# Weight operands kept in DRAM as one F32 part, split on load, with a respread decoding

## The chip, the cores and the metric

The kernel runs on one core of one Trainium2 chip. The metric is device time in microseconds, the median of the runs; less is better.

## The reference, cut to what matters

```python
# attention with decay: B=4, H=8, S=768, D=64, gamma[h] = 1 - 2**(-5-h)
for t in range(S):
    state = gamma[None, :, None, None] * state + np.einsum('bhd,bhe->bhde', k[:, :, t], v[:, :, t])
    y[:, :, t] = scale * np.einsum('bhd,bhde->bhe', q[:, :, t], state)
x = y.transpose(0, 2, 1, 3).reshape(B * S, H * D)        # 3072 x 512
h = (x @ w1) * (x @ w2)                                  # 512 -> 1024
x = h @ w3 @ w_out                                       # 1024 -> 1024 -> 512
h = x @ w_in                                             # 512 -> 2048
return (h * (1 / (1 + np.exp(-1.702 * h)))) @ w_out2     # 2048 -> 512
```

Inputs q, k, v are F32. The weights come as 64-bit floats and are decoded to F32 on the chip.

## The kernel before, in words

**Arithmetic.** A product is taken with three matmuls (`mm3`, L248 to L251): an operand is held as a high part, rounded to fp32r, and a low part, the residue, and high x high, high x low and low x high are summed. A split is a ScalarE cast and a VectorE subtraction (`split`, L263). The three large products behind the gates use seven block products in place of eight (P1 to P7): a 2 x 2 block operand is turned into seven operands by subtractions.

**Decoding.** `tiles` (L89) lists 36 weight tiles of 128 x 1024: 8 of w1 and w2, 4 of w_out, 8 of w3, and 16 of the FFN (w_in, then w_out2). Each half (512 columns) is fetched on SyncE's queue (`fetch`, 0.5 MB, `R_BUFS` = 4 buffers "r"), turned into a magnitude by ScalarE (`magnitude`, L114, 4 buffers "x"), then by VectorE through a clamp (L189), a shift (L198) and two bit merges (L202, L214). `weight_steps` is a generator with a yield after each step; `work(n)` takes n steps, as long as `done` is below `limit`. A tile of the first 20 is split into high and low on the chip and takes 10 steps. A tile of the FFN goes to `seven` (L158): POOL forms four differences (`four`, L144), ScalarE casts the seven parts, VectorE takes their residues (11 steps with these), and `store_parts` (L132) stores high and low parts to the DRAM tensors `sp` (w_in) or `sw` (w_out2), four stores on SyncE's queue.

**Stages.** Tokens are in six blocks of 512. (1) Attention, chunk by chunk, with the gates of block 0 between; decoding may take 86 steps here. (2) The mixed stage (loop at L989): for blocks n = 1 to 5 in `ORDER`, eight gates each (`gate_mm`, 24 matmuls of 512 columns), with PSUM for three gates. Between the gates of n = 1 and at the first of n = 2 stand eight rows of w3 @ w_out (`mix_mm`, 24 matmuls each); `mix_out` forms their seven parts per pair of rows, splits them, and stores them to `sm`. Decoding goes on: 8 steps per gate and 7 per row up to `limit` = 206 steps, then 5 per gate. Blocks 0 to 2 of `ORDER` store their gate products to `hd` (`gate_first`); blocks 3 to 5 read them back (`load_b`) and form five further operands by four POOL subtractions (L985), stored to `hd` on SyncE's queue (`gate_second`). In the last block `opening` loads the mixed weights, high and low, for each of the seven products, and the first operands of the next stage.

(3) The blend (`blend`, L783), 21 turns of 24 matmuls (three block pairs times seven products): `load_turn` fetches an operand of `hd` (1 MB, buffers "l", 3) on SyncE's queue two turns ahead, a split gives its high part (buffers "h", 2), TensorE multiplies, ScalarE, VectorE and POOL combine the results, which go to `yd` on SyncE's queue. `ahead` takes four decoding steps per turn while tiles are left; later it forms the operands of the next stage. (4) The expand (`Expand`, L525): left operands are the eight tiles of `sp`, fetched by POOL's queue (`fetch_left`, high and low, 1.8 MB each) into slots 0 to 7; four spans of 2 x 384 tokens, eight quads each, a quad being 42 matmuls of 384 columns; results go through the activation and to `gd`. (5) The contract (`contract`, L694), 21 turns of 48 matmuls: operands of `gd` are loaded and split per turn, weights of `sw` are loaded per product by `load_w`, high and low into two slots.

**Order.** The schedule is written by hand: each engine and each queue runs its instructions in the order in which the program gives them. A buffer with n copies is reused in turn, after the readers of its last content are done. A pool opened over another's room waits for what lay there.

## Time and profile before

| | us |
|---|---|
| median of 3 runs (lowest, highest) | 1085.14 (1082.16, 1089.9) |
| the profiled execution | 1086.86 |
| its span, first to last instruction | 1085.1 |
| TensorE busy in the span | 995.1 |
| VectorE, ScalarE, POOL busy | 715.4, 458.2, 186.9 |

The profile is of one execution. DMA moved 305.44 MB, a mean of 281 GB/s, and TensorE's mean granted clock was 0.964 of 2.4 GHz. The attention ends at about 150 us, the mixed stage runs from there to 439, the blend to 607, the expand to 852 and the contract to the end.

### The profile page before, as it was taken

What the parts mean: (1) busy time and instruction counts of PE and PEld (TensorE: products, weight loads), DVE (VectorE), ACT (ScalarE), POOL (GpSimd) and SP (SyncE); (2) the same over time, 40 slices, a digit from 0 to 9 for tenths busy, and PEclk for the clock granted to TensorE, in tenths of its full rate; (3) what the DMA queues carried; (4) which work ended last, traced back from release to release, by engine and by line L of the source; (5) the groups of instructions that cost most, each with busy time, mean ns of one, the idle gap of its engine ahead of it and who ended that gap; (6) DMA issues with size and microseconds to landing.
All of it is one profiled execution on the core that took longest, in us unless ns stands there. A gap on an engine that the chain in (4) does not pass through costs nothing.

```text
span 1085.1 us, 15024 instructions
## 1 busy us (share of the span) xinstructions
PE 995.1 (92%) x5608; PEld 852.0 (79%) x5608; DVE 715.4 (66%) x964; ACT 458.2 (42%) x831; POOL 186.9 (17%) x188
## 2 busy tenths in 40 slices
PE   4899899999999896568789889999999999999998
PEld 4788678778887774456577779999999888888886
DVE  5767768887799996338277238677677545455562
ACT  4556645444423332144434234544454543343340
POOL 3101000214377675314011100000000000000000
PEclk9999899999999997779899999999999999999999
DMA  8789947668899989998876695554659797887881
GB/s 309 244 315 342 338 170 236 222 218 275 324 367 323 379 320 394 415 343 275 282 234 199 262 414 232 214 233 192 231 215 367 296 371 241 290 300 261 283 269 62
DMA packets 140009, 305.44 MB, mean 281 GB/s; under 512 B 8480, under 2 KB 91552, under 8 KB 128544
## 3 DMA queue, kind: packets, MB, share of 16 engines
q1 hardware_dynamic: 133600, 253.89, 65.6%
q0 software_dynamic: 6336, 50.60, 12.3%
q8 instruction: 44, 0.72, 0.3%
q14 instruction: 29, 0.24, 0.1%
HBM read 183.87 MB, written 120.59 MB: 281 GB/s over the span
## 4 chain that ended last, share of the span: by engine, by line
PE 60%; DMA 19%; DVE 12%; issue 4%; ACT 4%; POOL 0%; SPq 0%; ACTq 0%; DVEq 0%; POOLq 0%
PE m L250 9%; PE m L251 8%; PE m L249 8%; DMA l<-hd 5%; PE a L249 4%; PE a L251 4%; PE a L250 4%; DMA raw<-in_wo_dram 4%; DMA xl<-xd 2%; DVE x L214 2%; PE e L251 2%; PE e L249 2%; PE e L250 2%; ACT h L264 2%; DVE x L202 2%
## 5 line engine op out<-in xcount | busy, mean ns | idle before, releaser
L249 PE MATMUL psm<-xh,wh 128*128 128x512 f32 x320 | 127.1, 397 | 15.3 <-ACT g L287 11.4
L250 PE MATMUL psm<-xl,wh 128*128 128x512 f32 x320 | 126.2, 394 | 0.0
L251 PE MATMUL psm<-xh,wl 128*128 128x512 f32 x320 | 126.0, 394 | 0.0
L249 PE MATMUL m<-h,op 128*128 128x512 f32 x320 | 124.5, 389 | 0.0
L251 PE MATMUL m<-h,op 128*128 128x512 f32 x320 | 124.5, 389 | 0.0
L250 PE MATMUL m<-l,op 128*128 128x512 f32 x304 | 118.3, 389 | 0.0
L664 ACT CAST h<-l 128x2048 fp32r<-128x2048 f32 x38 | 72.3, 1914 | 93.3 <-DMA l<-gd 49.2
L665 DVE TENSOR_TENSOR l<-l,h 128x2048 fp32r<-128x2048 f32 x38 | 85.8, 2286 | 28.6 <-ACT h L664 28.6
L249 PE MATMUL a<-yh,op 128*128 128x384 f32 x256 | 86.6, 338 | 7.9 <-ACT u L536 4.8
L250 PE MATMUL a<-yl,op 128*128 128x384 f32 x256 | 86.3, 337 | 0.0
L251 PE MATMUL a<-yh,op 128*128 128x384 f32 x256 | 86.3, 337 | 0.0
L249 PE MATMUL m<-h,wh 128*128 128x512 f32 x166 | 69.7, 420 | 17.8 <-ACT h L264 17.8
L249 PEld LDWEIGHTS psm<-xh,wh 128*128 128x128 f32 x320 | 61.0, 191 | 30.9 <-ACT g L287 12.2
L121 ACT ACTIVATE x<-raw 128x512 f32<-128x512 f32 x72 | 47.1, 673 | 90.3 <-DMA raw<-in_wo_dram 50.2
L156 DVE TENSOR_TENSOR l<-l,h 128x2048 fp32r<-128x2048 f32 x19 | 44.2, 2325 | 56.3 <-ACT h L264 56.3
L250 PE MATMUL m<-l,wh 128*128 128x512 f32 x152 | 62.8, 413 | 13.7 <-DVE l L156 13.6
L670 POOL DMA_DIRECT2D op<-sw x12 | 6.3, 528 | 399.5 <-PE a L251 222.0
L251 PEld LDWEIGHTS psm<-xh,wl 128*128 128x128 f32 x320 | 61.0, 191 | 13.1
L250 PEld LDWEIGHTS psm<-xl,wh 128*128 128x128 f32 x320 | 61.1, 191 | 12.5
L249 PEld LDWEIGHTS m<-h,op 128*128 128x128 f32 x320 | 60.1, 188 | 12.6
L251 PEld LDWEIGHTS m<-h,op 128*128 128x128 f32 x320 | 60.1, 188 | 12.3
L251 PE MATMUL m<-h,wl 128*128 128x512 f32 x166 | 68.6, 414 | 0.0
(147 smaller groups left out, 2222.8 us busy)
## 6 DMA issues: line engine op xcount, KB each, us to landing
gd<-g SPq DMA_DIRECT2D x32, 1344.0 KB, 5.1
qkv<-in_qkv_dram POOLq DMA_DIRECT2D x23, 1024.0 KB, 8.3
l<-gd SPq DMA_DIRECT2D x26, 768.0 KB, 7.1
l<-hd SPq DMA_DIRECT2D x19, 1024.0 KB, 6.6
raw<-in_w_dram SPq DMA_DIRECT2D x32, 512.0 KB, 5.3
hd<-g SPq DMA_DIRECT2D x12, 1280.0 KB, 6.8
op<-sp POOLq DMA_DIRECT2D x7, 1792.0 KB, 16.5
raw<-in_wo_dram SPq DMA_DIRECT2D x24, 512.0 KB, 8.6
```

What stands on the lines that cost most here:

```text
L121: nc.scalar.activation(x, high, AF.Abs, scale=2.0**16)
L156: nc.vector.tensor_tensor(lo, x, hi.bitcast(F32), ALU.subtract)
L202: nc.vector.scalar_tensor_tensor(bits, raw[:, :, 0], 29, bits, ALU.logical_shift_right, ALU.bitwise_or)
L214: nc.vector.scalar_tensor_tensor(bits, raw[:, :, 1], -(2**31), bits, ALU.bitwise_and, ALU.bitwise_or)
L249: nc.tensor.matmul(ps, wh, xh, start=start, stop=False, skip_group_check=True)
L250: nc.tensor.matmul(ps, wh, xl, start=False, stop=False, skip_group_check=True)
L251: nc.tensor.matmul(ps, wl, xh, start=False, stop=stop, skip_group_check=True)
L264: nc.scalar.copy(hi, x)
L664: nc.scalar.copy(hi, x.bitcast(F32))
L665: nc.vector.tensor_tensor(x, x.bitcast(F32), hi.bitcast(F32), ALU.subtract)
L670: queue.dma_start(t.bitcast(F32), sw[PART[name], :, w])
```

## The change

Weight parts go through DRAM as F32, undivided: `sp`, `sw` and `sm` lose their high and low halves. Where they are loaded, ScalarE and VectorE split them: left tiles in the first span of the expand (`split_left`), contract weights in every third turn (`split_w`), mixed weights at the last two gates and the first turns of the blend (`split_wm`). An FFN tile then has 8 steps; `limit` is lifted at the start of the mixed stage, and the steps per gate are 8 up to n = 2, 3 for n = 3 and 4, and 1 for n = 5. There are five raw buffers (three in use from n = 4 on, so that the operand h1 fits into two), six "x" and four "l" buffers. Stores of parts, of g and of yd move from SyncE's queue to POOL's; two of the four subtractions of `gate_second` move from POOL to VectorE, one of them to the gate before. The next block's x is loaded at gates 0 and 1 and split at 4 to 7.

```diff
-R_BUFS = 4
+R_BUFS = 5
...
-    sp = spool("sp", NQ, P, 2, 7 * 256)
-    (sw,) = spool("sw", 1, 7, P, 2, NQ, 256)
-    (sm,) = spool("sm", 1, 7, P, 2, NM, 256)
+    sp = spool("sp", NQ, P, 7 * 256)
+    (sw,) = spool("sw", 1, 7, P, NQ, 256)
+    (sm,) = spool("sm", 1, 7, P, NM, 256)
...
-    def fetch(n):
-        i, c = divmod(n, 2)
-        if i >= len(tiles):
+    fetched = used = 0
+    allowed = R_BUFS
+    def fetch():
+        nonlocal fetched
+        if fetched >= min(used + allowed, 2 * len(tiles)):
             return
+        i, c = divmod(fetched, 2)
+        fetched += 1
...
-            x = prep.tile([P, WC], F32, tag="x", bufs=4, name="x")
...
+            x = prep.tile([P, WC], F32, tag="x", bufs=6, name="x")
...
-    def store_parts(i, m, hi, lo):
-        a, b = (0, 3) if m == 0 else (3, 7)
-        for n, x in enumerate((hi, lo)):
-            x = x[:, : (b - a) * 256]
+    def store_parts(i, a1, a2, st):
+        for a, x in ((0, a1), (2, a2[:, 256:]), (3, st)):
+            b = a + x.shape[1] // 256
             if WI <= i < WI + NQ:
-                to = sp[i - WI][:, n, a * 256 : b * 256]
+                to = sp[i - WI][:, a * 256 : b * 256]
...
                 to = (sm, i) if i < WI else (sw, i - WI - NQ)
-                to = to[0][a:b, :, n, to[1]].rearrange("r p c -> p r c")
+                to = to[0][a:b, :, to[1]].rearrange("r p c -> p r c")
                 x = x.rearrange("p (r c) -> p r c", c=256)
-            nc.sync.dma_start(to, x.bitcast(F32))
+            nc.gpsimd.dma_start(to, x)
...
-    def seven(i):
...
+    def seven(i, a1, a2):
+        st = homes["st"].tile([P, 1024], F32, tag="st", bufs=2, name="st")
         four(st, a1, a2)
-        h0, l0, h1, l1 = (tile(F32R) for _ in range(4))
-        nc.scalar.copy(h0[:, :512], a1)
-        nc.scalar.copy(h0[:, 512:768], a2[:, 256:])
-        def last():
-            nc.scalar.copy(h1, st)
-            residue(h1, l1, st)
-            store_parts(i, 1, h1, l1)
-        def second():
-            residue(h0[:, 512:768], l0[:, 512:768], a2[:, 256:])
-            store_parts(i, 0, h0, l0)
-        return [lambda: residue(h0[:, :512], l0[:, :512], a1), second, last]
+        store_parts(i, a1, a2, st)
...
                     upper(i, n)
-                elif n:
-                    lows[:] = seven(i)
-                fetch(2 * i + n + R_BUFS)
-                yield i
+                used += 1
+                fetch()
+                fetch()
+                magnitude(i + 1)
+                if i >= WI and n:
+                    seven(i, *wx[i])
+                yield i + (i >= WI and n)
...
     def fetch_left(n, queue=nc.gpsimd):
...
+        t = left[n][:, 1].rearrange("p b c -> p (b c)")
+        queue.dma_start(t.bitcast(F32), sp[n])
+    def split_left(n):
+        hi, lo = (left[n][:, w].rearrange("p b c -> p (b c)") for w in range(2))
+        split(hi, lo, lo.bitcast(F32))
...
             next(fourth)
+            if s == 0 and j + 2 < NQ:
+                split_left(j + 2)
...
             self.results = [self.result(j) for j in range(2)]
+            split_left(1)
...
-    def load_w(name, w, at, queue=nc.gpsimd):
+    def load_w(name, at, queue=nc.gpsimd):
         t = slot(at, [P, NQ, 256])
-        ws.setdefault(name, []).append(t)
-        queue.dma_start(t.bitcast(F32), sw[PART[name], :, w])
+        ws[name] = [None, t]
+        queue.dma_start(t.bitcast(F32), sw[PART[name]])
+    def split_w(name, at, a=0, b=NQ, copy=nc.scalar.copy):
+        if a == 0:
+            ws[name][0] = slot(at, [P, NQ, 256])
+        hi, lo = (x[:, a:b] for x in ws[name])
+        copy(hi, lo.bitcast(F32))
+        nc.vector.tensor_tensor(lo, lo.bitcast(F32), hi.bitcast(F32), ALU.subtract)
...
     OPENING = {(n + 1, 1): [lambda n=n: opening_slot(n)] for n in range(4)}
+    OPENING[5, 1] = [lambda: load_w("P1", 4)]
     for n in range(2):
-        OPENING[5 + n, 1] = [lambda n=n: load_w("P1", n, 4 + n)]
+        OPENING[6, 1 + 2 * n] = [
+            lambda n=n: split_w("P1", 5, n * KH, n * KH + KH, nc.vector.tensor_copy)
+        ]
...
             if i == 0 and r + 1 < 7:
-                for w in range(2):
-                    queue = nc.gpsimd if r else nc.sync
-                    load_w(turns[n + 3][0], w, (6, 4)[r % 2] + w, queue)
+                load_w(turns[n + 3][0], (6, 4)[r % 2], nc.gpsimd if r else nc.sync)
...
             split_turn(n + 1, p)
+            if i == 1 and r + 1 < 7:
+                split_w(turns[n + 2][0], (7, 5)[r % 2])
...
-    def load_h(n, t):
+    def load_h(n, a, b, t):
         i, name = blends[n]
-        lo2[n] = t
-        nc.sync.dma_start(t.bitcast(F32), hd[i][:, :, RIGHT[name]])
...
+        lo2.setdefault(n, []).append((a, b, t))
+        nc.sync.dma_start(t.bitcast(F32), hd[i][:, a:b, RIGHT[name]])
+    def low_h(n, k):
+        return next(t[:, k - a] for a, b, t in lo2[n] if a <= k < b)
+    def split_h(n, a, b, hi):
+        for c, d, t in lo2[n]:
+            c0, d0 = max(a, c), min(b, d)
+            if c0 < d0:
+                lo = t[:, c0 - c : d0 - c]
+                split(hi[:, c0 - a : d0 - a], lo, lo.bitcast(F32))
+    wm = {}
+    def split_wm(n):
+        hi, lo = wm[blends[n][1]]
         split(hi, lo, lo.bitcast(F32))
...
             wm[name] = wtile("wg")
...
+            nc.sync.dma_start(
+                wm[name][1].bitcast(F32), sm[PART[name]].rearrange("p k c -> p (k c)")
+            )
...
             hi2[0] = x[:, NM:]
-            load_h(0, x[:, :NM])
-            load_h(1, prep.tile([P, NM, TB], F32R, tag="h1", name="h1"))
+            load_h(0, 0, NM, x[:, :NM])
+        if t == KF - 2:
+            for k in (0, 2):
+                load_h(1, k, k + 2, prep.tile([P, 2, TB], F32R, tag="r", bufs=R_BUFS, name="h1"))
         if t in (4, 5, 6):
-            split_h(0, t - 4)
+            split_h(0, t - 4, t - 3, hi2[0][:, t - 4 : t - 3])
+        if t in (6, 7):
+            split_wm(t - 6)
...
             if n < len(blends):
-                load_h(n, tile("l", 3))
+                load_h(n, 0, NM, tile("l", 4))
...
         def store(i, e, t):
-            nc.sync.dma_start(yd[i][:, e], t)
+            nc.gpsimd.dma_start(yd[i][:, e], t)
...
         load_turn(2)
-        hi2[1] = tile("h", 2)
+        hi2[1], k3 = tile("h", 2), tile("h", 2)[:, 0]
+        load_turn(3)
...
         ready = [value()]
-        k3 = p.tile([P, TB], F32R, name="k3")
-        split(k3, lo2[0][:, 3], lo2[0][:, 3].bitcast(F32))
+        split_h(0, 3, 4, k3.rearrange("p (a t) -> p a t", a=1))
...
             if n:
-                load_turn(n + 2)
+                load_turn(n + 3)
...
                         k3 if (n, k) == (0, 3) else hi2[n][:, k],
-                        lo2[n][:, k],
+                        low_h(n, k),
...
                     hi2[n + 1] = tile("h", 2)
-                split(hi2[n + 1], lo2[n + 1], lo2[n + 1].bitcast(F32))
+                split_h(n + 1, 0, NM, hi2[n + 1])
+            if n + 2 < 7:
+                split_wm(n + 2)
...
             pb = stage.enter_context(tc.tile_pool(name="b1", bufs=1, reuse_waits="tile"))
-            homes["wa"] = homes["wc"] = pb
-            limit = TILE_OPS * WI + 6
+            homes.update(dict.fromkeys(("wa", "wc", "st"), pb))
+            limit = ALL
...
                 if f % 2 == 0:
-                    pair = pb.tile([P, 2, 2, 256], F32, tag="xp", name="xp")
+                    pair = pb.tile([P, 2, 2, 256], F32, tag="xp", bufs=2, name="xp")
                 nc.scalar.copy(pair[:, :, f % 2], ps.rearrange("p (m f) -> p m f", m=2))
-                if f % 2 == 0:
-                    return
-                a1, a2 = (pair[:, m].rearrange("p a f -> p (a f)") for m in range(2))
-                st = pb.tile([P, 1024], F32, tag="st", name="st")
-                four(st, a1, a2)
...
-                    for r, x in todo:
-                        split(hi[:, r], lo[:, r], x)
-                    store_parts(f // 2, m, hi, lo)
-                pieces(0, [(slice(512), a1), (slice(512, 768), a2[:, 256:])])
-                later.append(lambda: pieces(1, [(slice(1024), st)]))
+                if f % 2:
+                    seven(f // 2, *(pair[:, m].rearrange("p a f -> p (a f)") for m in range(2)))
...
             def gate_second(t, i, ab):
-                nonlocal b12
+                nonlocal b12, g
+                b = hb[0]
...
                     b12 = pb.tile([P, TB], F32, tag="b", bufs=2, name="b12")
+                    g = pb.tile([P, 5, TB], F32, tag="g", bufs=2, name="g")
                     gate_out(b12, ab)
+                    nc.vector.tensor_tensor(g[:, 1], b12, b[:, 0], ALU.subtract)
                     return
-                g = pb.tile([P, 5, TB], F32, tag="g", bufs=2, name="g")
                 gate_out(g[:, 0], ab)
-                b = hb.pop(0)
-                for x, y, z in (
-                    (1, b12, b[:, 0]),
-                    (2, g[:, 0], g[:, 1]),
-                    (3, g[:, 0], b12),
-                    (4, b[:, 1], g[:, 2]),
-                ):
-                    nc.gpsimd.tensor_tensor(g[:, x], y, z, ALU.subtract)
-                nc.sync.dma_start(hd[i // 2][:, t // 2, 2:], g)
-            b12 = pb2 = None
+                nc.vector.tensor_tensor(g[:, 3], g[:, 0], b12, ALU.subtract)
+                nc.gpsimd.tensor_tensor(g[:, 2], g[:, 0], g[:, 1], ALU.subtract)
+                nc.gpsimd.tensor_tensor(g[:, 4], b[:, 1], g[:, 2], ALU.subtract)
+                nc.gpsimd.dma_start(hd[i // 2][:, t // 2, 2:], g)
+                hb.pop(0)
...
                         opening(t)
-                    elif 1 <= t <= KD:
-                        reload(nxt, t - 1)
+                    elif t < 2:
+                        for d in range(2):
+                            reload(nxt, 2 * t + d)
...
                     ab = gate_mm(t, i, gate_tile)
-                    if nxt is not None and 3 <= t < 3 + KD:
-                        split_x(nxt, t - 3)
-                    end = t >= KF - 3 and nxt is None
-                    for _ in range(5 if pb2 else 8):
-                        before = complete
-                        work(1)
-                        if end and complete > before:
-                            limit = done
+                    if nxt is not None and t >= KD:
+                        split_x(nxt, t - KD)
+                    if n >= 4 and t > 2:
+                        allowed = R_BUFS - 2
+                    work((1 if nxt is None else 3) if n > 2 else 8)
                     (gate_second if n > 2 else gate_first)(t, i, ab)
...
                         if rows == KF:
-                            later.pop()()
                             stage.close()
-                            pb = pb2 = stage.enter_context(
+                            pb = homes["st"] = stage.enter_context(
...
                             )
-                            homes["wa"] = pb
-                            limit = ALL
...
             nonlocal py, early
+            if n == len(blends) - 2:
+                split_left(0)
```

## Rows read from the trace of the kernel before

**Rows 1.** The page, 40 slices of 27.1 us: TensorE busy, DMA busy, in tenths
```profile
PE   4899899999999896568789889999999999999998
...
DMA  8789947668899989998876695554659797887881
```

**Rows 2.** Windows by stage: us, busy us of each engine (instructions), PEclk, DMA, GB/s
```profile
151.00:288.00 137.00, 133.78 (x581) 109.94 (x582) 109.76 (x189) 63.27 (x106) 26.15 (x28) 0.99 0.72 250
288.00:440.00 152.00, 136.66 (x579) 110.64 (x578) 134.88 (x147) 49.51 (x84) 102.57 (x83) 0.94 0.96 352
439.00:607.00 168.00, 130.70 (x503) 101.14 (x503) 90.49 (x79) 63.97 (x66) 29.78 (x25) 0.89 0.79 277
607.00:661.00 54.00, 46.09 (x244) 45.06 (x243) 19.26 (x36) 19.82 (x44) 3.17 (x6) 0.94 0.92 375
661.00:852.00 191.00, 191.00 (x1104) 191.00 (x1103) 139.82 (x255) 94.02 (x210) 1.06 (x2) 1.00 0.62 239
```

**Rows 3.** Windows, instructions on tile m alone, late blend and contract
```profile
540.00:607.00 67.00, 60.49 (x261) 48.26 (x260) 5.12 (x8) 7.62 (x14) 1.00 0.61 200
852.00:1081.00 229.00, 228.68 (x1008) 189.17 (x1008) 20.00 (x29) 7.06 (x12) 1.00 0.79 267
```

**Rows 4.** Chain that ended last, in order of time: start, us, what
```profile
444.10 9.59 DMA sw<-ws
...
453.77 19.36 DMA l<-hd
...
547.64 6.22 DMA l<-hd
...
607.84 9.00 DMA op<-sp
```

**Rows 5.** Waits in the blend: who for whom, us, times, longest
```profile
PE m L249 <- ACT h L264: 17.8, 6, 7.7
...
PE m L250 <- DVE l L156: 13.6, 9, 1.8
...
ACT h L264 <- DMA l<-hd: 47.2, 11, 11.0
```

**Rows 6.** Lines of VectorE, 152 to 182 us: group xcount | busy us, mean ns
```profile
L202 DVE SCALAR_TENSOR_TENSOR x<-raw,x 128x512 int32<-128x512 int32 x8 | 5.1, 682 | 0.0
...
L198 DVE TENSOR_SCALAR x<-x 128x512 int32<-128x512 int32 x8 | 3.0, 418 | 0.0
```

**Rows 7.** Lines of VectorE, 300 to 400 us
```profile
L202 DVE SCALAR_TENSOR_TENSOR x<-raw,x 128x512 int32<-128x512 int32 x14 | 16.7, 1227 | 0.0
...
L198 DVE TENSOR_SCALAR x<-x 128x512 int32<-128x512 int32 x14 | 14.1, 1040 | 0.0
```

**Rows 8.** DMA issues: op xcount, KB each, us to landing
```profile
l<-hd SPq DMA_DIRECT2D x19, 1024.0 KB, 6.6
...
op<-sp POOLq DMA_DIRECT2D x7, 1792.0 KB, 16.5
...
sp<-ws SPq DMA_DIRECT2D x16, 512.0 KB, 7.5
```

**Rows 9.** Lines of the whole span
```profile
L664 ACT CAST h<-l 128x2048 fp32r<-128x2048 f32 x38 | 72.3, 1914 | 93.3 <-DMA l<-gd 49.2 <-PE m L251 41.8 <-DVE l L665 2.3
...
L665 DVE TENSOR_TENSOR l<-l,h 128x2048 fp32r<-128x2048 f32 x38 | 85.8, 2286 | 28.6 <-ACT h L664 28.6
...
L153 POOL TENSOR_TENSOR ws<-x 128x256 f32<-128x256 f32 x32 | 29.5, 922 | 86.5 <-DVE x L214 59.4 <-issue 20.2 <-ACT ws L167 4.9
...
L985 POOL TENSOR_TENSOR g<-h,g 128x512 f32<-128x512 f32 x12 | 19.9, 1661 | 0.0
...
L156 DVE TENSOR_TENSOR xl<-xl,xh 128x512 fp32r<-128x512 f32 x20 | 14.8, 739 | 7.5 <-ACT xh L264 7.3
...
L330 POOL DMA_DIRECT2D qkv<-in_qkv_dram x25 | 14.0, 562 | 100.1 <-ACT state L386 25.4 <-PE y L408 21.3 <-ACT wh L125 18.1
```

**Rows 10.** Timeline of SyncE's queue: start, us, what
```profile
464.99 13.78 SPq L142 DMA_DIRECT2D sw<-ws  x2
```

More of the change, by code (lines that the diff above doesn't have):

```diff
@@ L116, in magnitude @@
             return
-        wx[i] = []
-        for raw in raws[i]:
-            x = prep.tile([P, WC], F32, tag="x", bufs=4, name="x")
+        xs = wx.setdefault(i, [])
+        for raw in raws.get(i, [])[len(xs) :]:
+            x = prep.tile([P, WC], F32, tag="x", bufs=6, name="x")
             high = raw[:, :, 1].bitcast(F32)
             nc.scalar.activation(x, high, AF.Abs, scale=2.0**16)
-            wx[i].append(x)
+            xs.append(x)
     def upper(i, n):
@@ L204, in weight_steps @@
                 )
-                yield i - len(rest)
-            for f in rest:
-                f()
                 yield i
@@ L518, in fetch_left @@
     def fetch_left(n, queue=nc.gpsimd):
-        t = left[n]
-        queue.dma_start(t.rearrange("p a b c -> p a (b c)").bitcast(F32), sp[n])
+        t = left[n][:, 1].rearrange("p b c -> p (b c)")
[3 more added lines that the diff above has]
+        split(hi, lo, lo.bitcast(F32))
     def left_parts(n, name, k):
@@ L770, in opening @@
             wm[name] = wtile("wg")
-            for w, x in enumerate(wm[name]):
-                nc.sync.dma_start(
-                    x.bitcast(F32), sm[PART[name], :, w].rearrange("p k c -> p (k c)")
-                )
+            nc.sync.dma_start(
+                wm[name][1].bitcast(F32), sm[PART[name]].rearrange("p k c -> p (k c)")
+            )
         if t == 1:
@@ L922, in tile_kernel @@
             psw = mixed_bank()
-            later = []
             rows = 0
@@ L1014, in tile_kernel @@
                         work(7)
-                        while later:
-                            later.pop()()
                         mix_out(rows, ps)
@@ L1019, in tile_kernel @@
                         if rows == KF:
-                            later.pop()()
                             stage.close()
-                            pb = pb2 = stage.enter_context(
+                            pb = homes["st"] = stage.enter_context(
                                 tc.tile_pool(name="b2", bufs=1, reuse_waits="tile")
                             )
-                            homes["wa"] = pb
-                            limit = ALL
         inner.close()
-        limit = ALL
-        homes["wa"] = second.enter_context(
+        homes["st"] = second.enter_context(
             tc.tile_pool(name="wa", bufs=1, side="right", reuse_waits="tile")
```

35 lines of the change are left out of this document (11 added, 24 removed).

## Prediction

> **What bounds the kernel now.** I read the page's slices first: TensorE is at 9 nearly everywhere but the start, a stretch in the middle and a few single slices, and the dip lies where DMA is at 8 to 9 [rows 1]. Next come windows by stage [rows 2] and the pace where nothing waits, the contract: 228.68 us for 1008 matmuls [rows 3], 0.227 us each, so 5.44 us for the 24 matmuls of a gate, a mixed row or a blend turn. The expand's pace is 191 us for 1104 [rows 2], 0.173 each, 7.27 us a quad of 42. Against these paces the stages lose:
> - 151 to 288 us (16 gates and 8 mixed rows of blocks n = 1 and 2, 24 x 5.44 = 130.7): 137 - 130.7 = 6.3;
> - 288 to 440 (24 gates, n = 3 to 5): 152 - 130.7 = 21.3, at a DMA share of 0.96;
> - 439 to 607 (blend, 21 turns, 114.3): 53.7;
> - 607 to 661 (244 matmuls, 5.8 quads, 42.2): 11.8. From 661 us on, nothing.
> Together 93.1 us; a change in the middle can win no more.
>
> What ends last there: the chain in order of time passes from a store of weight parts (9.59 us) into the blend's first loads of hd (19.36), later from load to load (6.22), and into the expand by a load of left parts of 9.00 us [rows 4]. In the blend TensorE waits for splits by ScalarE (17.8) and VectorE (13.6), and ScalarE in turn 47.2 us for the loads [rows 5]. SyncE's queue is part of it: one pair of stores of parts, whose data was late, held it 13.78 us while the next load stood behind [rows 10]. So the bound from 288 to 660 us is transfers and the queue in front of them, with VectorE close behind (134.88 of 152 us busy [rows 2]).
>
> **The change, part by part.** *Traffic.* A tile of seven parts is 128 x 1792 F32, 0.92 MB; it went out and came back twice over and now goes once: 16 tiles to sp and sw and 4 to sm, both ways, 40 x 0.92 = 36.7 MB less. Per gate in n = 3 and 4 before: 5 of 11 steps, 0.45 tile x (1.05 read + 1.84 stored) = 1.31 MB, and g, h and x 1.05 MB: 2.36 MB in 5.44 us, 433 GB/s, against 352 reached [rows 2]; n = 5 also fetched two operand tiles per mix. After, a tile has 8 steps and a gate 3 of them: 0.37 x 1.97 + 1.05 = 1.78 MB, 328 GB/s; n = 5 (one step, half the mixed weights, two hd loads) 1.63 MB, 299 GB/s. Both lie below what the stage reaches now.
>
> *VectorE and POOL in n = 3 to 5.* The two residues of a tile leave VectorE, two subtractions per pair of gates come to it at 0.74 each [rows 9], and POOL loses those two at 1.66 [rows 9]. The two engines slow each other: the same shifts and ORs take 418 and 682 ns where POOL rests [rows 6], 1040 and 1227 where it is busy [rows 7]. VectorE per gate: 3 steps x 0.55 to 1.13, two products and a subtraction and half a split together 1.9: 3.6 to 5.3 us, inside 5.44 even at the dear end. I leave 4 us of the 21.3 (0 if all fits, 12 if stores and g still collide): gain 17.
>
> *Blocks n = 1 and 2.* The limit on decoding falls. By the step counts (86 done in the attention, 8 per gate, 7 per row) eight FFN tiles are now decoded in n = 2, one per gate, where three were. Per gate VectorE has 4 x 0.42 + 4 x 0.68 = 4.4 plus 1.05 for a product and a half split: 5.5 us; with all steps as dear as in rows 7 it is 4 x 1.04 + 4 x 1.23 + 1.05 = 10.1. POOL has four subtractions at 0.92 and three stores at 0.56 [rows 9], 5.4 us. DMA has 2.36 MB, 433 GB/s again. An x buffer now stays taken until its store has landed, 3.7 + 0.6 + 7.5 [rows 8] = 11.8 us after the tile, and six buffers want it back after two tiles. I take 6.3 us, near the cheap end, since POOL no longer works on g in this block: 8 x 0.86 = 7 us behind, of which the three pairs of PSUM banks hide most; 4 reach TensorE (none to 8 x 4.7 - 10.9 = 26). The mixed rows lose four splits of ScalarE and VectorE each pair: 2 back. The stage then loses 8: gain -2.
>
> *Blend.* Decoding is over but for two steps (before, seven turns carried it). The operand load is issued three turns ahead over four buffers, on a queue with no stores: it has 10.9 us for a landing of 6.6 [rows 8], and the 47.2 us of waits should go. What is late next is the split: a copy out of PSUM of 0.6, cast 1.91 and residue 2.29 [rows 9] follow the end of a turn, 4.8 us and the signals, against 5.44. So 21 turns cost between 5.44 and what the late turns cost now, 67 x 24 / 261 = 6.16 [rows 3]; I take the middle, 5.8, 121.8 us. The mixed weights' splits (ScalarE half of 1.91 and VectorE half of 2.29 in turns 0 to 4) fit beside it: ScalarE then has 4.1 of 5.44, VectorE 5; without that cover they cost up to 5 x 1.1. One wait is new: k3 now takes the second "h" buffer, so the operand of turn 2 gets the one that turn 1 reads, and its split starts when turn 1 ends: 4.9 once (nothing, if that turn's load is late anyway). Left over 12.4 of 53.7: gain 41 (24 to 50).
>
> *Expand.* Left tiles 1 to 6 are 5.5 MB instead of 11. But the split of tile 1 stands on ScalarE ahead of quad 0's copies. Tile 1 landed after 9.00 us [rows 4], the middle one after 16.5 [rows 8]; at half the bytes I estimate 5.5. Then the cast of 1792 columns, 7/8 of 1.91, 1.7 us, and a copy of 0.5: TensorE, done with P1 and P5 after 2.1, waits until 7.7 + 0.6 (issue) = 8.3, 6.2 us lost, where 2.7 were lost before. The other 9 us, late tiles and stores of g held up at 375 GB/s [rows 2], fall to about 2. The later splits (1.7 of ScalarE, 2.0 of VectorE in a quad of 7.27 in which they are busy some 3.6 and 5.3 [rows 2]) fit. Left over 8.5 of 11.8: gain 3 (-3 to 8).
>
> *Contract.* A split of 1.91 and 2.29 in every third turn: 191 us of the expand and all of the contract run without loss and with both engines below 0.75 busy; the split is due two turns ahead. Nothing, and at most 6 x 0.5 without cover. *Startup.* A fifth raw buffer asks for 0.5 MB more beside the first qkv loads: 1.4 us at 370 GB/s lost, or as much won later from being further ahead; nothing, give or take 2.
>
> *Store queue.* Stores move to POOL at 0.56 us an issue [rows 9], in order with its arithmetic. The operands' stores wait there for POOL's own results, and behind them stand only POOL's next tile and g. In n = 3 to 5 POOL has 7 x (3.7 + 1.7) + 12 x (3.3 + 0.6) = 85 of 131 us.
>
> **The sum.** -2 + 17 + 41 + 3 = 59, with 1 us less of low clock after stalls (0.89 granted in the blend [rows 2]) 60. The profiled execution took 1086.9 (1.8 around its span of 1085.1), the median of the runs is 1085.1, 1.7 below; 1085 - 60 = **1025 us**. About 1% is what a measurement of this kernel tells from no change.
>
> One rule speaks against the new queue. By the Trainium skill (SBUF — State Buffer, "A bandwidth-pool intuition that's wrong (but worth ruling out)"), a DMA issued by POOL can take 3.1 us instead of 0.62 beside a VectorE copy, since its descriptors wait for the shared port. By that price the third rival below would come out at 1111 us. This trace disagrees so far: 25 issues by POOL beside decoding took 562 ns in the mean [rows 9], but those are loads, and no row has a store.
>
> **Rivals.**
> *The blend keeps its pace.* The split chain of 4.8 us plus signals, not the loads, sets the turn, and the first loads come late because their buffers lie over g, whose last store must land first. Turns of 6.16 [rows 3] and 10 us at the start: 129.4 + 10 + 4.9 = 144, 18 more than forecast: 1043. For it: 13.6 us of waits for VectorE in nine short pieces [rows 5]. Against: those fell in turns whose load was late.
> *Block n = 2 is overloaded.* VectorE at 10.1 us a tile: 26 instead of 4: 1047. For it: rows 7. Against: there POOL was 102.57 of 152 us busy [rows 2], mostly with g.
> *POOL's queue sets the pace, and the kernel is slower.* If a store takes s us of POOL, n = 2 has 8 x (3.7 + 3s) against 43.5 and 10.9 of slack, and n = 3 to 5 have 65.7 + 33s against 130.7; the loss is 57s - 90, which eats the gain from s = 2.6 on; at s = 3 it is 81 us: 1106. For it: stores have up to 512 pieces instead of 128. Against: 0.56 [rows 9], and left loads of 256 pieces cost POOL no more.
> *The transfers were hidden anyway*, and only order changes: n = 3 to 5 are held by POOL and VectorE, and half the blend's loss stays: 1060. Against: 0.96 DMA share [rows 2] and the chain [rows 4].
>
> **Chances.** Forecast 0.66, blend's pace 0.13, n = 2 0.09, hidden transfers 0.07, POOL's queue 0.05. The range goes from 1004 (blend 50, n = 3 to 5 all 21, expand 8, first blocks 2) to 1060, which holds the first two rivals and leaves out the last, and what lies above the one before. Faster by over 1% (below 1074): all cases but POOL's queue, less a little, 0.92; within 1% 0.03; slower 0.05.
>
> **What would show it.** Right: DMA share from 288 to 440 us at about 0.8, gates of 5.44; no decoding beside the blend and ScalarE's wait for hd near 5 us; turn 2 late by 5; a stall of 6 us in quad 0, none from quad 1 on; contract unchanged; total traffic near 269 MB. Wrong: TensorE waiting in n = 2 for the products' VectorE steps, POOL DMA issues far above 0.6 us, or VectorE's residue still behind TensorE in every blend turn.

## Result and the profile after

The changed kernel takes 1016.72 us (median of four runs, 1016.0 to 1019.8), the kernel before 1085.39 in the same comparison: ratio 0.937, 95% interval 0.9331 to 0.9409. That is 68.7 us less, where 60 were forecast, inside the range. The profiled execution took 1016.0 us with a span of 1014.2, and TensorE's mean granted clock rose from 0.964 to 0.984.

The page of the kernel after: 40 slices of 25.4 us, TensorE busy, its granted clock and DMA in tenths, what DMA moved, and the chain's shares by engine.

```profile
PE   4999999999989999899997999999999999999998
...
PEclk9899999999989999999997999999999999999999
DMA  8789956569999977998846745546497978767871
...
DMA packets 115032, 268.73 MB, mean 265 GB/s; under 512 B 7952, under 2 KB 69520, under 8 KB 105488
...
PE 82%; DVE 5%; DMA 4%; POOL 4%; issue 3%; ACT 2%; POOLq 0%; DVEq 0%; ACTq 0%; SPq 0%
```

Against [rows 1] the dip in the middle is gone. Four notches are left, at slices 12, 17, 22 and the start; slice 12 is block n = 3's first gates, slice 17 (406 to 431 us) the blend's first turn, slice 22 (533 to 558) the expand's first quad. The traffic is the 269 MB of the forecast, 36.7 less than before. On the chain of work that ended last, transfers fell from 19% to 4% and TensorE rose from 60% to 82%.

Windows by stage, with the columns of [rows 2]: n = 1 and 2; the first 10 us of n = 3; n = 3 to 5 and what follows them up to the blend; the blend's first turns; the rest of the blend; the first of the expand.

```profile
147.00:278.00 131.00, 131.00 (x578) 108.37 (x579) 117.22 (x190) 51.37 (x89) 59.01 (x70) 1.00 0.74 252
278.00:288.00 10.00, 5.37 (x17) 3.65 (x16) 10.00 (x16) 2.85 (x6) 6.36 (x9) 0.74 1.00 365
278.00:415.00 137.00, 132.37 (x573) 108.78 (x572) 110.88 (x130) 32.90 (x58) 89.37 (x96) 0.98 0.88 320
415.00:440.00 25.00, 19.90 (x80) 15.67 (x79) 19.74 (x18) 12.61 (x14) 11.51 (x12) 0.93 0.96 362
440.00:537.00 97.00, 97.00 (x429) 80.07 (x428) 69.22 (x51) 48.93 (x45) 23.18 (x29) 1.00 0.72 249
537.00:591.00 54.00, 46.74 (x254) 46.34 (x253) 32.32 (x44) 31.17 (x52) 3.68 (x7) 0.91 0.68 261
```

Waits of TensorE from 147 to 600 us, as in [rows 5]: who for whom, us in total, times, longest.

```profile
PE a L232 <- ACT s L523: 7.3, 1, 7.3
PE m L233 <- DVE h L160: 4.0, 1, 4.0
PE psm L232 <- ACT xh L247: 3.6, 1, 3.6
PE m L233 <- DVE l L160: 1.1, 1, 1.1
PE psm L233 <- DVE xl L160: 1.0, 1, 1.0
```

Between three single stalls (278 to 288, at 415, at 538) TensorE hardly waits: 131.00 us busy of 131 for the first 24 gates and rows, where the pace alone asks 130.7, and 97.00 of 97 us busy in the late blend, 429 matmuls, 5.43 us per 24. Where ScalarE waited 47.2 us for hd in the blend [rows 5], the same group has 2.2 now.

The stages of each run, in one profiled execution: the attention up to the first gate matmul behind it, each later stage up to the start of its last matmul. The last columns are the median of all runs and its ratio to the kernel before. This table carries the experiments below; two profiles with the same code in a stage differ by up to 3 us there (the expand of e1 and of the changed kernel).

| kernel | attention | mixed | blend | expand | contract | median | ratio |
|---|---|---|---|---|---|---|---|
| before | 150.9 | 287.7 | 168.8 | 244.7 | 228.5 | 1085.39 | |
| after | 146.9 | 268.6 | 121.9 | 243.7 | 228.4 | 1016.72 | 0.937 |
| e1 | 146.0 | 278.4 | 122.2 | 240.9 | 228.5 | 1025.01 | 0.9441 |
| e2 | 146.8 | 285.7 | 138.1 | 246.3 | 228.5 | 1053.35 | 0.9706 |
| e3 | 145.5 | 274.6 | 123.5 | 243.5 | 228.5 | 1022.75 | 0.9422 |
| e4 | 145.8 | 271.5 | 129.8 | 242.9 | 228.4 | 1024.93 | 0.9448 |
| e10 | 147.0 | 268.5 | 123.3 | 242.8 | 228.5 | 1019.05 | 0.9393 |
| e5 | 147.0 | 269.2 | 122.2 | 243.4 | 228.4 | 1013.60 | 0.9336 |
| e6 | 147.0 | 268.9 | 120.4 | 250.9 | 228.5 | 1023.18 | 0.9423 |
| e8 | 147.7 | 266.0 | 126.7 | 242.6 | 228.4 | 1016.91 | 0.9362 |
| e9 | 150.3 | 280.7 | 122.1 | 243.3 | 228.5 | 1031.32 | 0.9503 |
| e7 | 147.3 | 277.6 | 126.0 | 242.3 | 228.5 | 1028.15 | 0.9464 |
| b1 | 151.0 | 308.4 | 150.1 | 246.2 | 228.5 | 1089.44 | 1.0025 |
| e12 | 146.6 | 270.2 | 126.5 | 240.4 | 228.5 | 1018.66 | 0.9382 |

### The profile page after: what moved, and what is told of

Its sections match the earlier page's. It is cut to its first block, busy times and chain, and to the rows that moved or that the text cites. A ratio compares the mean times of both kernels' runs of the same rounds, so it can differ in the third digit from the quotient of the medians.

```text
span 1014.2 us, 14850 instructions
## 1 busy us (share of the span) xinstructions
PE 971.7 (96%) x5608; PEld 841.1 (83%) x5608; DVE 727.0 (72%) x954; ACT 448.8 (44%) x793; POOL 209.8 (21%) x254
## 4 chain that ended last, share of the span: by engine, by line
PE 82%; DVE 5%; DMA 4%; POOL 4%; issue 3%; ACT 2%; POOLq 0%; DVEq 0%; ACTq 0%; SPq 0%
PE m L233 11%; PE m L234 11%; PE m L232 11%; PE psm L233 5%; PE psm L234 5%; PE psm L232 5%; PE a L232 4%; PE a L233 4%; PE a L234 4%; PE e L233 2%; PE e L234 2%; PE e L232 2%; POOL st L157 2%; PE s L331 2%; PE y L381 2%
## 5 line engine op out<-in xcount | busy, mean ns | idle before, releaser
L660 POOL DMA_DIRECT2D op<-sw x6 | 3.2, 530 | 400.1 <-PE a L234 219.7
L232 PEld LDWEIGHTS psm<-xh,wh 128*128 128x128 f32 x320 | 60.6, 189 | 16.7 <-ACT xh L247 4.0
L233 PEld LDWEIGHTS m<-l,op 128*128 128x128 f32 x304 | 57.1, 188 | 11.9
L232 PE MATMUL m<-h,wh 128*128 128x512 f32 x168 | 66.1, 393 | 0.0
L234 PE MATMUL m<-h,wl 128*128 128x512 f32 x168 | 65.9, 392 | 0.0
```

Of the source, the lines that this page charges most:

```text
L232: nc.tensor.matmul(ps, wh, xh, start=start, stop=False, skip_group_check=True)
L233: nc.tensor.matmul(ps, wh, xl, start=False, stop=False, skip_group_check=True)
L234: nc.tensor.matmul(ps, wl, xh, start=False, stop=stop, skip_group_check=True)
L660: queue.dma_start(t.bitcast(F32), sw[PART[name]])
```

## Experiments

All but b1 start from the changed kernel, and "more" or "less" is against its 1016.72 us.

**e1: the three kinds of stores back on SyncE.**

```diff
-            nc.gpsimd.dma_start(to, x)
+            nc.sync.dma_start(to, x)
...
-            nc.gpsimd.dma_start(yd[i][:, e], t)
+            nc.sync.dma_start(yd[i][:, e], t)
...
-                nc.gpsimd.dma_start(hd[i // 2][:, t // 2, 2:], g)
+                nc.sync.dma_start(hd[i // 2][:, t // 2, 2:], g)
```

> The changed kernel with its three kinds of store (weight parts, g, yd) back on SyncE's queue. Theory (a store whose data is late holds the loads behind it): raw loads of block n = 2 and operand loads of the blend come late again; 5 us in the mixed stage and 3 in the blend, about 1025 us (1020 to 1032). Rival (the queue only changes who issues): within 3 us of 1017, or faster, since POOL loses some 0.6 us a store.

Measured: 8.3 us over the changed kernel (interval of the ratio 0.9425 to 0.9457); in the stages it is the mixed one that grows (+9.8), and the blend, which has yd's stores, is unchanged. Windows of e1, at the start of n = 3, where the changed kernel has 15.37 us of 20 busy:

```profile
278.00:298.00 20.00, 10.55 (x33) 6.80 (x32) 19.63 (x30) 6.88 (x12) 8.87 (x12) 0.75 0.95 330
```

What SyncE's queue waited for from 250 to 300 us, and ScalarE for raw weights there, in e1; the last row's group has 8.1 us (2 times) in the kernel after.

```profile
SPq L146 <- POOL st L157: 9.2, 6, 2.8
...
SPq L116 <- DVE x L197: 9.1, 10, 2.6
...
ACT x L126 <- DMA raw<-in_wi_dram: 20.9, 4, 11.5
```

The first row is the stores of a tile (L146): they stand in the queue until POOL's differences are done, and the next loads of raw weights (L116) stand behind them. The second row is loads that wait for a raw buffer to come free; the changed kernel has that too (16.9 us, 8 times), so it isn't the stores' doing. The queue matters, at the place where most tiles are decoded.

**b1: the same three stores moved to POOL in the kernel before.**

```diff
-            nc.sync.dma_start(to, x.bitcast(F32))
+            nc.gpsimd.dma_start(to, x.bitcast(F32))
...
-            nc.sync.dma_start(yd[i][:, e], t)
+            nc.gpsimd.dma_start(yd[i][:, e], t)
...
-                nc.sync.dma_start(hd[i // 2][:, t // 2, 2:], g)
+                nc.gpsimd.dma_start(hd[i // 2][:, t // 2, 2:], g)
```

> The kernel before with nothing but the stores of parts, g and yd moved to POOL's queue. Theory (bytes are the bound there, the queue alone frees little): 1079 us (1070 to 1090). Rival (loads held up behind stores on SyncE's queue were the blend's loss): 1060 or less, the blend 20 us shorter.

Measured: ratio 1.0025 (1.0005 to 1.0046), so no gain. The blend wins 18.7 us and the mixed stage loses 20.7. Waits of TensorE in b1, from 147 to 600 us:

```profile
PE psm L249 <- ACT g L287: 17.3, 2, 16.7
PE m L249 <- ACT h L264: 13.7, 1, 13.7
```

ScalarE's waits for hd in the blend, 47.2 us before [rows 5], are 26.1 in b1 (459 to 610 us). That fits stores in SyncE's queue, as the pair of [rows 10], having been a brake on the blend; but the longer mixed stage also gave the transfers more time ahead of it, and this run doesn't part the two. Without the rest of the change the time came back ahead of the blend, most of it as one gate's wait of 16.7 us.

**e2: the traffic of before, the rest of the change kept.** Each part is stored into two planes and both are loaded, the second into the room of the high part, where the split then overwrites it (the contract's P1 is loaded once).

```diff
-    sp = spool("sp", NQ, P, 7 * 256)
+    sp = spool("sp", NQ, P, 2, 7 * 256)
...
+            for w in range(2):
+                v = x
...
-                to = sp[i - WI][:, a * 256 : b * 256]
+                    to = sp[i - WI][:, w, a * 256 : b * 256]
...
-            nc.gpsimd.dma_start(to, x)
+                nc.gpsimd.dma_start(to, v)
...
```

> The changed kernel with the old traffic: each part is stored twice into two planes and both planes are loaded, the second over the place that the split then fills (three more POOL issues of 0.6 to 0.8 us a tile come with it). Theory (bytes were the bound from 288 to 660 us): block n = 2 goes to 3.3 MB a gate, 8 us; n = 3 to 5 to 390 GB/s; the left tiles land late again; about 20 us more, 1037 (1027 to 1052). Rival (the bytes were hidden, order and steps did it): at most 5 us more, 1017 to 1022.

Measured: 36.6 us more, with 17 in the mixed stage, 16 in the blend, 3 in the expand. Windows of e2, from n = 3 to the end of the mixed stage:

```profile
278.00:432.00 154.00, 136.10 (x573) 110.57 (x574) 103.21 (x136) 34.98 (x61) 115.07 (x139) 0.93 0.98 367
```

DMA is at 0.98 and 367 GB/s, above the 0.96 and 352 of the kernel before [rows 2], where the changed kernel has 0.88 and 320. TensorE's longest waits are 10.2 us for a cast of a blend operand and 9.6 in the first quad. Half of what the change won is given up. Not all of that need be bytes: e2 also issues three more stores a tile on POOL, which is busy 115.07 us here. But where ScalarE waits long for anything other than TensorE at the end of the mixed stage, in the blend and in the first quads, it is for transfers. Waits of ScalarE in e2 from 425 to 640 us:

```profile
ACT h L249 <- DMA l<-hd: 13.7, 2, 11.9
ACT g L272 <- DMA hd<-g: 13.0, 1, 13.0
...
ACT h L249 <- DMA h<-hd: 11.8, 2, 11.6
```

In the changed kernel the same three are 2.2, 10.4 and 2.8 us (405 to 600 us), and e2's one wait for POOL's arithmetic there is 0.8.

**e3: the old limit and steps per gate** (eight, or five once the mixed rows are done).

```diff
-            limit = ALL
+            limit = TILE_OPS * WI + 6
...
-                    work((1 if nxt is None else 3) if n > 2 else 8)
+                    work(5 if rows == KF else 8)
...
                         if rows == KF:
+                            limit = ALL
                             stage.close()
```

> The changed kernel with the decoding spread as before: a limit of 206 steps until the mixed rows are done, then 5 steps a gate. Theory (spreading early pays, its price is the stall of some 7 us at the start of n = 3): that stall goes, but n = 3 and 4 carry 5 steps, 7 us of VectorE a gate against 5.44, and lose 10 to 15 us behind the PSUM slack: 1022 (1017 to 1030). Rival (eight steps a gate in n = 2 is too early, the old spread is as good now that a tile has 8 steps): 1010.

Measured: 6.0 us more, in the mixed stage. (The intervals of the two ratios just touch, 0.9406 to 0.9438 against up to 0.9409, but every run of e3 is above every run of the changed kernel.) Windows of e3, with the same stretches of the kernel after below:

```profile
278.00:298.00 20.00, 20.00 (x90) 16.53 (x90) 17.29 (x23) 5.68 (x10) 12.92 (x18) 1.00 0.95 337
318.00:338.00 20.00, 17.36 (x70) 13.84 (x69) 19.43 (x25) 3.73 (x7) 16.86 (x20) 0.91 0.89 289
358.00:378.00 20.00, 12.93 (x56) 10.11 (x55) 18.35 (x25) 4.38 (x9) 15.30 (x18) 0.89 0.72 241
```

```profile
278.00:298.00 20.00, 15.37 (x57) 11.88 (x56) 19.65 (x30) 5.96 (x11) 14.82 (x21) 0.83 0.93 332
318.00:338.00 20.00, 20.00 (x90) 16.57 (x89) 19.38 (x24) 3.76 (x7) 15.23 (x17) 1.00 0.87 304
358.00:378.00 20.00, 20.00 (x90) 16.57 (x89) 17.05 (x22) 3.36 (x6) 14.12 (x14) 1.00 0.74 258
```

The stall of n = 2's overload goes (20.00 instead of 15.37) and a dearer pair appears later, with VectorE at 18.4 to 19.4 of 20 us. Spreading the steps moves the stall to where it costs less; it doesn't remove it.

**e8: seven steps instead of eight in n = 2, and the last one in n = 5.**

```diff
-                    work((1 if nxt is None else 3) if n > 2 else 8)
+                    work((8, 7, 3, 3, 2)[n - 1])
```

> The changed kernel with 7 steps a gate in n = 2 in place of 8, and 2 in place of 1 in n = 5. Theory (eight steps put VectorE 13 us behind TensorE by the end of n = 2, two more than PSUM covers, and the last split for n = 3 comes late): the stall of 7 us at the start of n = 3 goes, 1010 us (1007 to 1014). Rival (the stall is the transfers', raw tiles come late at any pace): within 2 us of 1017.

Measured: 1016.91 us, 0.2 from the changed kernel. TensorE's waits at the start of n = 3, 4.6 us above, are 2.7, so the stall shrinks but doesn't go. The mixed stage is 2.6 us shorter and the blend 4.8 longer: the wait for VectorE at the first turn, 4.0 us above, is 5.3. The same finding as e3, from the other side.

**e4: loads two turns ahead over three buffers, as before.**

```diff
-                load_h(n, 0, NM, tile("l", 4))
+                load_h(n, 0, NM, tile("l", 3))
-        load_turn(3)
-                load_turn(n + 3)
+                load_turn(n + 2)
```

> The changed kernel with operand loads of the blend two turns ahead in three buffers, as before, all else new. Theory (depth of the loads is what freed the blend: a landing takes 6.9 us, a turn 5.44): each turn is 0.5 to 1 us longer, 1028 us (1023 to 1038). Rival (the blend was freed by the decoding that left it and by the stores that left the queue): within 3 us of 1017.

Measured: 8.2 us more, the blend 129.8. But most of the loss lies ahead of the first turn, not between the turns. Timeline of ScalarE in e4:

```profile
428.09 2.51 ACT L247 CAST h<-h 128x512 fp32r<-128x512 f32 x3 [12.46 <-DMA hd<-g]
```

The casts of the first operands waited 12.5 us for a store of g, and from 440 to 530 us TensorE has 87.87 us busy of 90, so some 2 us are lost between the turns. With one buffer fewer, the buffers allocated behind it lie elsewhere; the suspicion was that this place is room that g still held.

**e10: e4 with an unused buffer in front, so that the "h" buffers lie where the change has them.**

```diff
...
+        tile("pad", 1)
         hi2[1], k3 = tile("h", 2), tile("h", 2)[:, 0]
```

> The run before (operand loads two turns ahead, three buffers) with an unused tile of 8 KB a partition in the place of the fourth buffer, so that all other tiles of the blend's pool lie where they lie in the changed kernel. Theory now (what the fourth buffer gives is place: with three, the high part of turn 1 lies over the last g and waits 12.5 us for its store): back to 1017 us (1014 to 1020), blend 122 us. Rival (depth): it stays at 1025, blend 130.

Measured: 1019.05 us, 5.9 below e4, the blend 123.3. So of the fourth buffer's 8.2 us some 6 are its place in the memory. The 2.3 that are left for the third turn of advance aren't told from nothing (the intervals of e10, 0.9364 to 0.9422, and of the changed kernel overlap).

**e5: a third buffer for g.**

```diff
-                    g = pb.tile([P, 5, TB], F32, tag="g", bufs=2, name="g")
+                    g = pb.tile([P, 5, TB], F32, tag="g", bufs=3, name="g")
```

> The changed kernel with three buffers of g in place of two. Theory (in block n = 5 the first subtraction waits for a store of g, so VectorE comes late to the last split before the blend, and turn 0 waits 4.0 us): turn 0 loses 1 us or less, 1012 us (1009 to 1016). Rival (the transfers of the opening make VectorE late anyway): within 2 us of 1017.

Measured: 1013.60 us, 0.9336 (0.9309 to 0.9364). The wait of 4.0 us at the first turn falls to 0.9, and in its place TensorE waits 1.9 for ScalarE's cast and 1.9 for VectorE's residue of the operand; the blend is 122.2. (The profiled execution is the slowest of the four, 1016.70 us, so its stages don't show the gain of the median.) The cause of that wait is the right one; the gain isn't told from nothing, as the interval overlaps that of the change.

**e6: the split of a left tile one quad ahead instead of two.**

```diff
-            if s == 0 and j + 2 < NQ:
-                split_left(j + 2)
+            if s == 0 and j + 1 < NQ:
+                split_left(j + 1)
...
-            split_left(1)
```

> The changed kernel with the split of left tile n placed in quad n - 1 behind its second copy, tile 1 too, in place of ahead of quad 0 and in quad n - 2. Theory (the split of tile 1 holds the copies of quad 0 on ScalarE, 7.3 us): quad 0 runs through; quad 1 waits for tile 1 (landed 7.4 us after quad 0 begins, cast 1.7, residue 2.0), some 4 us; gain 3 us: 1014 (1011 to 1017). Rival (tile 1 ends last either way): within 1 us of 1017.

Measured: 6.5 us more, the expand 250.9. (The interval, 0.9401 to 0.9446, reaches into that of the change, but all four runs are above all of the changed kernel's.) Waits of TensorE in e6 from 530 to 800 us:

```profile
PE a L234 <- DVE op L160: 9.8, 7, 1.4
PE a L232 <- ACT op L247: 2.9, 1, 2.9
```

The one stall of 7.3 us becomes 2.9, and seven quads wait 1.4 each: the residue is issued in the quad before its use, behind the activation's work, and comes 1.4 us late. Two quads ahead is early enough and costs once.

**e9: four raw buffers again.**

```diff
-R_BUFS = 5
+R_BUFS = 4
```

> The changed kernel with four raw buffers (two in use from n = 4 on). Theory (the fifth buffer lets raw tiles come earlier: it gives the 4 us by which the attention ended earlier, and cover in n = 2): 1023 us (1019 to 1028), the mixed stage starting near 151 us instead of 147. Rival (the 4 us come from the six x buffers and the magnitudes taken one by one): the attention still ends at 147 and the time stays within 2 us of 1017.

With four, two buffers are in use from n = 4 on in place of three, so the edit bears on the end of the mixed stage too. Measured: 14.6 us more, the largest of the single edits but the traffic: attention back to 150.3 and 12.1 in the mixed stage. As the six x buffers stay, they are not what shortened the attention. ScalarE's waits for raw weights, e9 from 150 to 430 us and then the kernel after from 147 to 415:

```profile
ACT x L126 <- DMA raw<-in_wo_dram: 82.1, 20, 18.9
ACT x L126 <- DMA raw<-in_wi_dram: 20.8, 10, 4.3
```

```profile
ACT x L126 <- DMA raw<-in_wo_dram: 47.6, 9, 15.4
ACT x L126 <- DMA raw<-in_wi_dram: 13.6, 5, 4.3
```

**e7: all four subtractions of `gate_second` on POOL, as before.**

```diff
-                    nc.vector.tensor_tensor(g[:, 1], b12, b[:, 0], ALU.subtract)
...
-                nc.vector.tensor_tensor(g[:, 3], g[:, 0], b12, ALU.subtract)
+                nc.gpsimd.tensor_tensor(g[:, 1], b12, b[:, 0], ALU.subtract)
+                nc.gpsimd.tensor_tensor(g[:, 3], g[:, 0], b12, ALU.subtract)
```

> The changed kernel with all four subtractions of g on POOL again, at the odd gate. Theory (POOL takes 1.3 to 1.7 us for what VectorE does in 0.7, and each holds up the other): 24 subtractions more on POOL, 36 us, of which block n = 3 to 5 has room for most; 1021 us (1016 to 1028). Rival (VectorE, busy 0.8 of n = 3 to 5, is what is short): faster, 1012.

Measured: 11.4 us more: 9.0 in the mixed stage, 4.1 in the blend. Windows of e7:

```profile
278.00:420.00 142.00, 130.71 (x556) 106.56 (x555) 105.51 (x111) 30.89 (x55) 116.59 (x121) 0.95 0.85 304
```

POOL is busy 116.59 of 142 us, in the changed kernel 89.37 of 137, and the differences, g and the stores stand behind that work in its order.

**e12: e5, other steps per gate, and tile 1's split behind quad 0's first copies.**

```diff
-                split_left(j + 2)
+                split_left(j + 2 if j else 1)
...
+            if s == 0 and j == 0:
+                split_left(2)
...
-            split_left(1)
...
-                    g = pb.tile([P, 5, TB], F32, tag="g", bufs=2, name="g")
+                    g = pb.tile([P, 5, TB], F32, tag="g", bufs=3, name="g")
...
-                    work((1 if nxt is None else 3) if n > 2 else 8)
+                    work((8, 7, 3, 4, 1)[n - 1])
```

> A version put together from the runs: 7 steps a gate in n = 2 and 4 in n = 4, three buffers of g, and the splits of left tiles 1 and 2 both within quad 0. Theory: the stall at n = 3 falls from 7 to 2 us, turn 0's wait from 4 to 2, quad 0's 7.3 to 3 at quad 1: 1007 us (1003 to 1012). Rival (each stall moves to the next engine that is late): 1013 to 1017.

Measured: 1018.66 us, no gain. The expand has 240.4, 3.3 less than the changed kernel's: the wait of 7.3 us in quad 0 is gone, and two of 3.1 and 1.1 come in its place. That is little more than the scatter of this stage (e1 has 240.9 with the splits left where they were). The mixed stage has 1.6 more and the blend 4.6, where TensorE waits 4.3 us for casts of h. The stalls moved again.

## Why the prediction was right, and where it was not

The forecast was right in direction and cause and near in size: its gain was some 9 us too small. By stage, forecast and measured gain: attention 0 and 4.0, mixed 15 and 19.1, blend 41 and 46.9, expand 3 and 1.0, contract 0 and 0.1. Part of the closeness is luck, as the blend below shows: one stall that was priced didn't come, and another of like size, from another cause, did.

*Traffic.* Right. DMA's share in n = 3 to 5 is 0.88 (0.8 was named), and e2 with 304 MB goes back up to 0.98 and gives up 36.6 us. The rival of hidden transfers is out.

*VectorE and POOL in n = 3 to 5.* The 4 us left there were too many: by the windows above TensorE is busy 127.00 of the 127 us from 288 to 415. e7 shows that this hangs on the moved subtractions, 24 of them for 11.4 us; the forecast listed them (0.74 more on VectorE, 1.66 less on POOL) but gave them no share of the gain of their own.

*Blocks n = 1 and 2.* The step was right in kind, mis-sized in its term, "I take 6.3 us". Timeline of VectorE after: the split of x, once a gate, and the product of the last gate of n = 2.

```profile
270.32 0.68 DVE L160 TENSOR_TENSOR xl<-xl,xh 128x512 fp32r<-128x512 f32 x1
...
277.45 0.68 DVE L160 TENSOR_TENSOR xl<-xl,xh 128x512 fp32r<-128x512 f32 x1
...
284.51 0.68 DVE L160 TENSOR_TENSOR xl<-xl,xh 128x512 fp32r<-128x512 f32 x1
...
291.02 0.67 DVE L271 TENSOR_TENSOR h<-h,psm 128x512 f32<-128x512 f32 x1
```

VectorE's steps of a gate take 7.1 us, not 6.3, and eight gates fall 8 x 1.66 = 13 us behind instead of 7; the last product starts 13 us after that gate's matmuls ended (at 278). About 7 us reach TensorE, in one place, 278 to 288 us, where 17 matmuls run in place of 44; the three pairs of banks hide the rest. Of these 7, 4.6 are the waits above (3.6 and 1.0), near the 4 of the forecast; the rest is the clock behind them, 0.66 granted in the mean from 280 to 290 us. The 2 us lost to the mixed rows' splits did come back: 131.00 us of 131 are busy up to 278.

*Blend.* The middle pace of 5.8 was too dear: 5.43 from 440 us on, so the split chain of 4.8 us fits, and the rival of the blend's own pace is out. Three of its steps failed. First, "k3 now takes the second 'h' buffer, so the operand of turn 2 gets the one that turn 1 reads": turn 2's cast (timeline of ScalarE after) began at 427.76, when turn 0 had just ended and turn 1 ran:

```profile
427.76 1.92 ACT L247 CAST h<-l 128x2048 fp32r<-128x2048 f32 x1
```

So it didn't wait for the room that turn 1 read; with two such buffers it took the one that k3 had, so the copies were not reused in turn here, and the stall of 4.9 us didn't come. Second, a stall of that size came one step earlier, at turn 0, and by another cause. VectorE after, then TensorE:

```profile
408.44 0.69 DVE L977 TENSOR_TENSOR g<-b,h 128x512 f32<-128x512 f32 x1 [7.26 <-DMA hd<-g]
...
420.29 5.11 DVE L160 TENSOR_TENSOR h<-h,h 128x512 fp32r<-128x512 f32 x3
...
422.10 0.50 PE L233 MATMUL m<-h,wh 128*128 128x512 f32 x1 [3.97 <-DVE h L160]
```

The chain gives the store of g at 398.42, 9.83 us, as what VectorE waited for: g has two buffers, and the next g may not be written before the old one is out. VectorE is 7 us late from there, TensorE goes on at 422.10, when the first of these three residues, that of k3, is done, and turn 0 takes 11.3 us in place of 5.44: 4.0 of waiting and some 2 at a low clock (0.83 granted from 420 to 430 us). e5 takes away most of that wait, and others of 1.9 us take its place. Third, the forecast gave the pace to the load "issued three turns ahead over four buffers". By e4 and e10 most of the worth of the fourth buffer is where it puts the others.

*Expand.* The stall in quad 0 is there as worked out. Chain after, and the cast behind it on ScalarE's timeline:

```profile
539.05 5.78 DMA op<-sp
```

```profile
544.86 1.68 ACT L247 CAST op<-op 128x1792 fp32r<-128x1792 f32 x1 [6.63 <-DMA op<-sp]
```

5.78 for an estimate of 5.5, 1.68 for 1.7, a wait of 7.3 for 6.2. Behind it comes a low clock, which the forecast's terms for this stage don't have. Window after:

```profile
540.00:550.00 10.00, 3.02 (x9) 3.02 (x10) 2.03 (x1) 3.15 (x5) 2.21 (x5) 0.61 0.97 371
```

The expand has 243.7 us where 32 quads of 7.27 ask 232.6: 11.1 lost, of which 7.8 are waits (7.3 and one of 0.5) and by estimate some 3 the clock. The forecast left 8.5 (its own terms, 6.2 and 2, add up to 8.2). The late tiles are gone, as said; the gain is 1.0 instead of 3.

*Attention.* By e9 the largest miss: "nothing, give or take 2" for the fifth raw buffer, which was priced only at the start of the kernel, and it was worth 4.0 here and 12 more in the mixed stage. What it does shows at 121 to 131 us. ScalarE before, where line L121 makes a magnitude of raw weights and L386 copies the attention's state:

```profile
125.59 0.66 ACT L121 ACTIVATE x<-raw 128x512 f32<-128x512 f32 x1 [3.74 <-DMA raw<-in_wo_dram]
...
127.18 0.37 ACT L386 COPY state<-u 128x256 f32<-128x256 f32 x1
```

TensorE before, then after:

```profile
127.60 1.12 PE L374 MATMUL u<-vs,qkv 128*64 128x64 f32 x16 [2.91 <-ACT state L386]
```

```profile
125.16 0.69 PE L357 MATMUL u<-vs,qkv 128*64 128x64 f32 x16 [0.83 <-ACT state L369]
```

The late weights stop ScalarE, the copy of the state stands behind them in its order, and TensorE waits for the copy. After it the granted clock was 0.77 from 129 to 139 us before, and 1.00 after: the same group of y at L408 (L391 after) starts at 131.16 against 127.84, and its next at 141.12 against 137.12, the whole 4.0 us. In e9 the same happens at 98 us: ScalarE waits 3.85 for raw weights and TensorE 1.80 for the state. With four buffers (before, b1, e9) the attention takes 150.3 to 151.0 us, with five in the ten others and the changed kernel 145.5 to 147.7.

*Contract and store queue.* Nothing, as forecast. The third rival, POOL's queue, is out; stores of parts by POOL after (duration in ns, least, median, most):

```profile
L146 POOL DMA_DIRECT2D sp<-x x16: 542/573/797, 239.2 to 290.5; - x16
L146 POOL DMA_DIRECT2D sp<-st x8: 537/540/570, 240.3 to 291.0; - x8
...
L146 POOL DMA_DIRECT2D sw<-x x16: 557/654/822, 296.6 to 433.5; - x16
L146 POOL DMA_DIRECT2D sw<-st x8: 762/762/762, 298.0 to 434.1; - x8
```

0.54 to 0.82 us, far from the 2.6 at which it would have eaten the gain. The Trainium skill's 3.1 us (SBUF — State Buffer, "A bandwidth-pool intuition that's wrong (but worth ruling out)") isn't seen here for stores either. The Trainium skill's rule that other issuing engines save only the time of the issue (DMA: Bandwidth & Descriptors, "Issuing engines are not separate DMA queues") fits b1, which gains nothing. But e1 shows more: a load behind a store whose data is late waits with it, and putting the stores back cost 8.3 us in this kernel.

The parts undone one by one sum to 8.3 + 36.6 + 6.0 + 8.2 + 14.6 + 11.4 = 85 us, more than the whole 68.7: they act on stalls that they have in common, so no part has a share of its own. What stays open: which buffers' rooms e4 and e10 differ in was read from one wait, not from addresses; and e2 parts bytes from the issues of the added stores only by the DMA share and by what ScalarE waited for, where a store that POOL issues late lands late too.

## What to carry to other kernels

Where a stage stands at the DMA limit, cut the bytes first: the same change of queue was worth 8 us here with the bytes gone and nothing with them. Price one more buffer by all it touches: what it lets a load do earlier, what stands in order behind the instruction that waited for that load, and where it pushes the buffers allocated after it. Near the end of tuning, ask of each stall removed which one is next; e3, e8 and e12 each took one away or shrank it, and the time was lost again elsewhere.

## What the hardware showed that was not expected

- A DMA issue by POOL costs more with some stores than the 0.56 us of a load [rows 9]. In the medians above it is 0.54 for sp<-st and 0.57 for sp<-x, but 0.65 and 0.76 for sw<-x and sw<-st, whose rows are 1 KB.
- How dear VectorE's steps are beside POOL doesn't follow from POOL's busy share alone. From 200 to 278 us after, with POOL busy 55.94 of 78 us, the bit merge of [rows 6] (682 ns with POOL idle) took 896 in the mean; from 300 to 400 us after, with POOL busy for a smaller share, 66.47 of 100 us, it took 1281. POOL's work differs there (differences of 256 columns and stores against subtractions of 512 columns as well); no run here parts the two. Lines of VectorE after, 200 to 278 us:

```profile
L188 DVE SCALAR_TENSOR_TENSOR x<-raw,x 128x512 int32<-128x512 int32 x22 | 18.9, 896 | 0.0
```

- A TensorE wait of 2.9 us in the attention, where the changed kernel has 0.8, cost 4 us, with 10 us at a mean granted clock of 0.77 behind it.
